# First 256 columns of x for the first 512 tokens: plain load and TensorE transposes in place of two crossbar pieces

## Chip, cores, metric

One core of one Trainium2 chip. The metric is the device time of one execution in microseconds (us), as the median of the executions. The profile counts from its own first instruction and ends a little earlier: its span is some 1.7 us below the device time of the same execution. In profile lines PE is TensorE (PEld its weight loads), DVE is VectorE, ACT is ScalarE, POOL is GpSimd, and SPq and ACTq are the queues from which the sync and scalar engines issue transfers. PSUM is the memory that TensorE's results land in.

## The reference, cut to what matters

```
x = A_x                                   # 2048 tokens x 1024, bf16
g = sigmoid((x * gate_w).sum(-1))
a = linear attention of x with A_wqkv (phi(t) = elu(t) + 1 + 1e-6), then @ A_wo
b = sliding-window attention of x (8 keys, every second token) with B_wqkv, then @ B_wo
return g * a + (1 - g) * b
```

All the work hangs on projections of x. The kernel feeds TensorE with x transposed (`xT`: features on partitions, tokens along the row). The very first projection is `k = x @ wk` of the linear attention; nothing useful can run on TensorE before the first piece of `xT` and of the weights `WkA` is there.

## The kernel before

All of x comes transposed through the DMA crossbar (`dma_start_transpose`). The first 512 tokens come in pieces of 256 columns, so that the projection can start on the first 256 columns:

```python
def load_xT(k, t0, t1):                      # crossbar: columns 256k..256k+255 of token tiles t0..t1-1
    nc.sync.dma_start_transpose(out=xT[:, 2 * k:2 * k + 2, t0 * P:t1 * P],
                                in_=rows(x, t0 * P, t1 * P)[:, 2 * k * P:(2 * k + 2) * P])

def load_wk(eng, k, h):                      # the weights for these columns, half h of the outputs
    eng.dma_start(out=WkA[h][:, 2 * k:2 * k + 2, :], in_=A_wqkv[2 * k * P:(2 * k + 2) * P, ...]...)

ones = nc.const_aps.tensor(1.0, [P, P], BF16)
load_wk(nc.scalar, 0, 0)
first_act = ...                              # a one-element activation
load_wk(nc.scalar, 0, 1)
load_xT(0, 0, 2)
load_xT(0, 2, 4)
for k in range(1, 4):
    load_wk(nc.sync, k, 0)
    load_xT(k, 0, 4)
    load_wk(nc.sync, k, 1)
...                                          # the other tiles of xT, then x as rows, other weights
mask = consts.tile([P, S // 2], BF16, name="mask")
nc.gpsimd.memset(mask[:], 1.0)
...  nc.gpsimd.affine_select(out=dst, in_=dst, ...)      # keeps or fills elements by position: the window's mask, needed much later
```

TensorE meanwhile multiplies ones by ones (warm-ups, to bring its clock up), then runs the projection in four groups `k` of 16 matmuls into 8 PSUM banks:

```python
warm_up(37)
first = [bank_k(i) for i in range(8)]
for k in range(4):
    for half in range(2):
        for t in range(4):
            for kt in (2 * k, 2 * k + 1):
                project(first[4 * half + t], t, kt, half)     # 128x128 weights, 512 columns moving
            ...
```

The softmax here doesn't subtract the row's maximum and nothing guards it: scores larger than these inputs give would overflow.

## Time and profile before

| | before |
|---|---|
| device time, median of 4 runs | 472.21 us (472.08 to 472.3) |
| span of the profiled execution | 470.9 us |
| warm-ups on TensorE | 0.84 to 4.95 us |
| first useful matmul | 5.35 us |
| GpSimd's first affine-select | 9.45 us |

The lines behind this table stand in the prediction below. How to read it: TensorE (PE in the profile) is busy nearly everywhere, so the time is the moment of its first useful matmul plus a nearly constant rest.

### The profile page before, as it was taken

To read this page: it belongs to the slowest core of one execution; us is meant where nothing else is said; L and a number is where in the kernel's file an instruction comes from. 1 tells how busy PE (TensorE), PEld (TensorE's weight loads), DVE (VectorE), ACT (ScalarE), POOL (GpSimd) and SP (SyncE) were. 2 spreads that over 40 slices of the span, in tenths; PEclk is the share of its full clock that TensorE was granted. 3 is DMA by queue.
4 is the path that set the end of the run, shared out by engine and by line. 5 is a ranking of instruction groups with operands and counts; after the bars stand their busy time and mean duration, and the time that the engine had idled before them with its cause. 6 is when DMAs were issued, how large, how long until landed. Compare 5 with 4: busy or idle time off the path is not lost.

```text
span 470.9 us, 13162 instructions
## 1 busy us (share of the span) xinstructions
PE 465.3 (99%) x5735; PEld 269.8 (57%) x5765; DVE 275.3 (58%) x598; ACT 169.1 (36%) x276; POOL 15.3 (3%) x30
## 2 busy tenths in 40 slices
PE   8999999999999999999999999999999999999997
PEld 5444444445444444444888888888874444444444
DVE  0596689990219999999666676767660049800000
ACT  1343321102433333334555555555553134221121
POOL 3300000500000000000000000000000000000000
PEclk9999999999999999999999999999999999999999
DMA  8999970000644233627325523442463923211001
GB/s 202 226 243 375 348 237 0 0 1 0 204 136 134 81 141 123 155 97 251 105 55 108 108 59 82 101 92 59 88 167 74 213 78 79 71 53 45 34 33 46
DMA packets 98732, 55.40 MB, mean 118 GB/s; under 512 B 70130, under 2 KB 90610, under 8 KB 98674
## 3 DMA queue, kind: packets, MB, share of 16 engines
q1 hardware_dynamic: 93378, 49.87, 39.9%
q10 hardware_dynamic: 5296, 4.69, 2.9%
q8 instruction: 45, 0.74, 0.6%
q14 instruction: 13, 0.11, 0.1%
HBM read 26.10 MB, written 15.86 MB: 89 GB/s over the span
## 4 chain that ended last, share of the span: by engine, by line
PE 86%; SPq 10%; DMA 2%; issue 1%; DVE 0%; DVEq 0%
PE q_ps L390 26%; PE d_ps L596 12%; PE p_ps L294 12%; PE e_ps L596 11%; PE g_ps L233 11%; PE p_ps L330 9%; SPq L115 4%; SPq L81 3%; DMA WvB<-in_B_wqkv_dram 2%; PE po L470 2%; PE s2b L448 2%; SPq L94 1%; SPq L98 1%; SPq L89 1%; SPq L119 1%
## 5 line engine op out<-in xcount | busy, mean ns | idle before, releaser
L390 PE MATMUL q_ps<-xT,WqB 64*64 64x512 bf16 x1024 | 70.3, 377 | 0.0
L390 PE MATMUL q_ps<-xT,WkB 64*64 64x512 bf16 x1024 | 69.8, 376 | 0.0
L156 DVE TENSOR_SCALAR e<-e 128x512 f32<-128x512 f32 x64 | 27.0, 423 | 68.3 <-ACT e L155 68.3
L294 PE MATMUL p_ps<-WvB,xT 128*128 128x512 bf16 x250 | 56.9, 379 | 0.3
L182 PE MATMUL pk_ps<-WkA,xT 128*128 128x512 bf16 x251 | 55.6, 381 | 0.7 <-DMA xT<-in_A_x_dram 0.4
L233 PE MATMUL g_ps<-pk,xrow 128*128 128x512 bf16 x251 | 55.2, 379 | 0.3
L453 ACT ACTIVATE PT<-s2b 128x928 bf16<-128x928 f32 (+4 forms) x40 | 34.2, 856 | 50.0 <-PE s2b L448 49.0
L455 DVE TENSOR_TENSOR PT<-PT,mask 128x928 bf16<-128x928 bf16 (+4 forms) x40 | 23.6, 590 | 36.3 <-ACT PT L453 36.3
L390 PEld LDWEIGHTS <-WkB 64*64 64x64 bf16 x1024 | 40.4, 107 | 6.9 <-DMA vd<-tmp 0.2
L330 PE MATMUL p_ps<-WqA,xT 128*128 128x512 bf16 x188 | 43.2, 379 | 0.3
L596 PEld LDWEIGHTS <-pqT 128*128 128x128 bf16 x272 | 26.0, 98 | 29.6 <-issue 0.2
L596 PEld LDWEIGHTS <-OBT 128*128 128x128 bf16 x272 | 26.0, 98 | 29.4
L182 PEld LDWEIGHTS <-xT 128*128 128x128 bf16 x256 | 25.1, 98 | 31.0 <-DMA xT<-in_A_x_dram 0.7
L390 PEld LDWEIGHTS <-WqB 64*64 64x64 bf16 x1024 | 39.4, 107 | 5.6 <-DVE qz L430 0.2
L233 PEld LDWEIGHTS <-xrow 128*128 128x128 bf16 x256 | 25.0, 98 | 30.2
L294 PEld LDWEIGHTS <-xT 128*128 128x128 bf16 x256 | 24.9, 98 | 30.2 <-issue 0.5
L603 DVE TENSOR_SCALAR osb<-e_ps,omg 128x128 bf16<-128x128 f32 x1 | 0.4, 351 | 57.6 <-PE e_ps L596 57.6
L155 ACT ACTIVATE e<-pk_ps 128x512 f32<-128x512 f32 x32 | 18.9, 597 | 40.6 <-PE pk_ps L182 36.4
L470 PEld LDWEIGHTS <-PT 64*56 64x56 bf16 (+2 forms) x1152 | 29.9, 104 | 4.5
L299 ACT CAST tmp<-p_ps 128x512 bf16<-128x512 f32 x32 | 18.7, 589 | 37.0 <-PE p_ps L294 26.6
L330 PEld LDWEIGHTS <-xT 128*128 128x128 bf16 x192 | 18.8, 98 | 22.6
L596 PE MATMUL d_ps<-WoA,pqT 128*128 128x512 bf16 (+1 forms) x133 | 30.7, 369 | 0.2
(63 smaller groups left out, 540.8 us busy)
## 6 DMA issues: line engine op xcount, KB each, us to landing
vd<-tmp SPq DMA_DIRECT2D x16, 264.0 KB
xrow<-in_A_x_dram SPq DMA_DIRECT2D x4, 1024.0 KB
out_dram<-osb ACTq DMA_DIRECT2D x31, 128.0 KB
pqd<-tmp SPq DMA_DIRECT2D x12, 256.0 KB
WvA<-in_A_wqkv_dram SPq DMA_DIRECT2D x2, 1024.0 KB
WoA<-in_A_wo_dram SPq DMA_DIRECT2D x2, 1024.0 KB
WvB<-in_B_wqkv_dram SPq DMA_DIRECT2D x2, 1024.0 KB
WqA<-in_A_wqkv_dram SPq DMA_DIRECT2D x2, 1024.0 KB
```

Source lines behind the costliest of these rows:

```text
L115: nc.sync.dma_start_transpose(out=xT[:, :, t * P:(t + 1) * P], in_=rows(x, t * P, (t + 1) * P))
L155: nc.scalar.activation(out=e[:], in_=pj[:], func=ACT.Exp)
L156: nc.vector.tensor_scalar(out=e[:], in0=e[:], scalar1=1.0, scalar2=1e-6, op0=ALU.min, op1=ALU.add)
L182: nc.tensor.matmul(pj[:], lhsT=xT[:, kt, t * P:(t + 1) * P], rhs=WkA[half][:, kt, :], start=(kt == 0), stop=(kt == KT - 1))
L233: nc.tensor.matmul(pj[:], lhsT=xrow[:, t, kt * P:(kt + 1) * P], rhs=pk[:, t, half * 512:(half + 1) * 512], start=(t == 0), stop=(t == NB - 1))
L294: nc.tensor.matmul(st["pj"][:], lhsT=xT[:, kt, t * P:(t + 1) * P], rhs=WvB[half][:, kt, :], start=(kt == 0), stop=(kt == KT - 1))
L330: nc.tensor.matmul(st["pj"][:], lhsT=xT[:, kt, t * P:(t + 1) * P], rhs=WqA[half][:, kt, :], start=(kt == 0), stop=(kt == KT - 1))
L390: nc.tensor.matmul(banks[o][64 * j:64 * j + 64, :], lhsT=lhsT(r, kt, j), rhs=rhs(r, kt), start=first and kt == 0, stop=kt == KT - 1, skip_ ...
L453: nc.scalar.activation(out=pt[:, :, 0:W_], in_=s2b[:].rearrange("p a b s -> p (a b) s")[:, :, 0:W_], func=ACT.Exp, scale=SCALE)
L455: nc.vector.tensor_tensor(out=pt[:, :, 0:W_], in0=pt[:, :, 0:W_], in1=mask[:, None, base:base + W_].broadcast_to([P, 4, W_]), op=ALU.mult)
L470: nc.tensor.matmul(o2[64 * h:64 * h + w, par, s_, i, :], lhsT=pt[r, i, o:o + w], rhs=V[r, m, 4 * c + i, :], start=True, stop=True)
L596: nc.tensor.matmul(st["ps"][:, 0:n], lhsT=lhsT, rhs=W[c0 // 512][:, c, c0 % 512:c0 % 512 + n], start=(side == 0 and c == 0), stop=(side == ...
```

## The change

Intent: get the first piece of `xT` without the crossbar. The first 256 columns of the first 512 tokens are loaded as plain rows; TensorE transposes them in eight 128x128 blocks against an identity matrix; DVE and ACT copy the blocks from PSUM into `xT`. The next crossbar piece goes ahead of the weights in the sync queue. Some warm-ups are taken out to make room. The diff, cut to its core (left out: a `load_rows` that takes a column range, so that the later load of these rows brings only the other 768 columns; one late weight load in two pieces):

```diff
     ones = nc.const_aps.tensor(1.0, [P, P], BF16)
+    pk = big.tile([P, NB, D], BF16, name="pk", tag="pkO")
+    ident = pk[:, NB - 1, 0:P]
+    nc.gpsimd.affine_select(out=ident, in_=ones, compare_op=ALU.is_equal, fill=0.0, base=0, pattern=[[1, P]],
+                            channel_multiplier=-1)
         load_wk(nc.scalar, 0, 0)
-        first_act = consts.tile([P, 1], BF16, name="first_act")
-        nc.scalar.activation(out=first_act[:], in_=ones[:, 0:1], func=ACT.Exp)
-        load_wk(nc.scalar, 0, 1)
-        load_xT(0, 0, 2)
-        load_xT(0, 2, 4)
-        for k in range(1, 4):
+        load_rows(nc.sync, 0, 4, 0, 2 * P)
+        load_xT(1, 0, 4)
+        load_wk(nc.sync, 0, 1)
+        load_wk(nc.sync, 1, 0)
+        load_wk(nc.sync, 1, 1)
+        for k in range(2, 4):
+            load_xT(k, 0, 4)
             load_wk(nc.sync, k, 0)
-            load_xT(k, 0, 4)
             load_wk(nc.sync, k, 1)
...
-            warm_up(37)
+            warm_up(33)
+            for t in (0, 2):
+                for kt in range(2):
+                    xt = ps_1.tile([P, 2 * P], BF16, name="xt_ps", tag="p1")
+                    for i in range(2):
+                        nc.tensor.transpose(xt[:, i * P:(i + 1) * P], xrow[:, t + i, kt * P:(kt + 1) * P], ident)
+                    (nc.scalar.copy if kt else nc.vector.tensor_copy)(out=xT[:, kt, t * P:(t + 2) * P], in_=xt[:])
```

More of the change, by code (lines that the diff above doesn't have):

```diff
@@ L86, with load_rows @@
     xrow = big.tile([P, NB, D], BF16, name="xrow", tag="vV")
-    def load_rows(eng, t0, t1):
-        eng.dma_start(out=xrow[:, t0:t1, :], in_=rows(x, t0 * P, t1 * P).rearrange("(t p) d -> p t d", p=P))
+    def load_rows(eng, t0, t1, d0=0, d1=D):
+        eng.dma_start(out=xrow[:, t0:t1, d0:d1],
+                      in_=rows(x, t0 * P, t1 * P)[:, d0:d1].rearrange("(t p) d -> p t d", p=P))
     WkA = [wpool.tile([P, KT, 512], BF16, name=f"WkA{h}", tag="wa") for h in range(2)]
@@ L115 @@
             nc.sync.dma_start_transpose(out=xT[:, :, t * P:(t + 1) * P], in_=rows(x, t * P, (t + 1) * P))
-        for t in range(0, NB, 4):
+        load_rows(nc.sync, 0, 4, 2 * P, D)
+        for t in range(4, NB, 4):
             load_rows(nc.sync, t, t + 4)
@@ L179 @@
             s1.enter_context(tc.manual_schedule(engines={DVE}))
-            pk = big.tile([P, NB, D], BF16, name="pk", tag="pkO")
             def project(pj, t, kt, half):
@@ L543 @@
             load_wo(1, 0, 4)
-            nc.sync.dma_start(out=WoB[1][:, 4:KT, :],
-                              in_=B_wo[4 * P:, 512:1024].rearrange("(k p) n -> p k n", p=P))
+            for k in (4, 6):
+                nc.sync.dma_start(out=WoB[1][:, k:k + 2, :],
+                                  in_=B_wo[k * P:(k + 2) * P, 512:1024].rearrange("(k p) n -> p k n", p=P))
             raw = wpool.tile([P, 4, D], BF16, name="raw", tag="wc")
```

## The prediction

> **What bounds the kernel now.** I read the page first, then the first 30 us in order of time, then the waits, then the last pieces of the chain. The page of the kernel before:
>
> ```profile
> span 470.9 us, 13162 instructions
> PE 465.3 (99%) x5735; PEld 269.8 (57%) x5765; DVE 275.3 (58%) x598; ACT 169.1 (36%) x276; POOL 15.3 (3%) x30
> PE   8999999999999999999999999999999999999997
> ...
> PE 86%; SPq 10%; DMA 2%; issue 1%; DVE 0%; DVEq 0%
> ```
>
> TensorE (PE) is busy in every slice and only the first and last slices are not full. The sum of its work is the span, so the change can act in two ways only: change how much PE does, or change when its first useful matmul starts. The list of PE waits shows that only the start is open (first for all of the run, then in the timeline of the start):
>
> ```profile
> PE warm L188 <- PEq L645: 0.8, 1, 0.8
> PE pk_ps L182 <- DMA xT<-in_A_x_dram: 0.4, 1, 0.4
> ```
>
> ```profile
> 0.80 0.95 POOL L129 MEMSET mask<- 128x1024 bf16 x1 [0.29 <-POOLq L645]
> ...
> 0.84 4.11 PE L188 MATMUL warm<-const-bfloat16-1.0 128*128 128x128 bf16 x37 [0.84 <-PEq L645]
> 1.69 0.14 POOL L141 MEMSET qsel<- 128x1 f32 x2
> ...
> 5.34 0.13 PEld L182 LDWEIGHTS <-xT 128*128 128x128 bf16 x2 [0.67 <-DMA xT<-in_A_x_dram]
> 5.35 24.99 PE L182 MATMUL pk_ps<-WkA,xT 128*128 128x512 bf16 x111 [0.40 <-DMA xT<-in_A_x_dram]
> ...
> 5.75 0.15 PEld L182 LDWEIGHTS <-xT 128*128 128x128 bf16 x1 [0.28 <-issue]
> 6.18 23.88 PEld L182 LDWEIGHTS <-xT 128*128 128x128 bf16 x111 [0.28 <-issue]
> ...
> 9.45 6.42 POOL L135 TENSOR_SCALAR_AFFINE_SELECT mask<-mask 64x64 bf16<-64x64 bf16 x15 [7.63 <-issue]
> ```
>
> Columns are start, duration, engine, line, operation, tiles and count, with the idle time before it. The reader is to see three things. PE multiplies constants (37 warm-up matmuls that produce nothing) from 0.84 to 4.95 us, then waits 0.40 us for the first crossbar piece of x, and does its first useful matmul at 5.35. After 6.18 it never waits. And GpSimd (POOL), which today has nothing to do with the start, stands idle from 1.83 to 9.45 us before its first affine-select although its input is ready: 7.63 us with the remark "issue", that is, nothing that the profile shows. At the end the chain is PE, then one small DVE evacuation:
>
> ```profile
> 467.23 0.91 PE e_ps L596 x16
> 468.14 0.04 DVEq L603
> 468.17 0.05 issue
> 468.22 0.35 DVE osb L603
> ```
>
> So: time = start of the first useful matmul (5.35) + about 463 us of dense PE + a fixed tail. A shift of the start goes through to the end one to one; I find no later wait that could swallow it. The most that an earlier start can bring is about 0.84 + 4.51 less what the first data need to arrive, and a quarter of a per cent is already 1.2 us.
>
> **What the Trainium skill says.** (1) "GPSIMD Engine Reference", section 2.1 Instruction dispatch: the GpSimd cores load kernel code at run time, and the first call into a freshly loaded kernel pays a load of some 6 us that no profile instruction shows. The trace agrees in kind and is longer: the 7.63 us above, in front of the first affine-select. In the built program an instruction that reloads the library stands just there, and the changed program has it in front of its very first affine-select. (2) "TensorE: Matmul & The Clock Gate", Part 1 (the HAM clock gate): PE runs at half clock until a free-running activity window of about 3.4 us has been busy, and falls back after an idle one. The trace agrees: 37 matmuls of 128 columns in 4.11 us are 111 ns each, while 111 of 512 columns in 24.99 us are 225 ns each, 56 ns per 128 columns; and the first useful loads start at 5.34, 5.75 and 6.18, so the first two useful matmuls still ran at the slow pace (about 0.41 us instead of 0.22, together 0.4 us lost). (3) The same page, Part 4 (PE-mode transpose): transposes do not count as busy for that gate. No row of the kernel before shows it, as it has none on PE. (4) "DMA: Bandwidth & Descriptors", Specifications: 512 B is the least run for full line rate. The plain load of 256 bf16 columns has runs of exactly 512 B, so it should not be penalised; no row of before has this size.
>
> **The change part by part.**
> Removed: two crossbar transposes of x (their issue held the sync queue from 0.81 to 3.42 us), a one-element activation, 4 of 37 warm-ups.
> Added: one plain load of 256 KB at 0.8 us; an identity made by an affine-select on POOL; 8 PE transposes; 4 copies of 128x256 out of PSUM, half on DVE, half on ACT.
> Moved: the next crossbar piece and the weights earlier in the sync queue by about 2 us. The second weight half goes from the ACT to the sync queue. Late weight halves in two pieces: 350 us later and with no wait there today, worth 0.
>
> Plain load: at 0.8 us with latency of issue about 2 us (the DMA slices of before are empty until about 2 us) and 512 KB of load and first weights at the 240 to 305 GB/s which the first slices reach, 1.7 to 2.2 us: x and the weights are there at about 4 us, 1.3 us earlier than today. If that were all: warm-ups end at 0.84 + 33 x 0.111 = 4.5; 8 transposes x 0.111 = 0.9 to 5.4; the first copies lie beside the later transposes; the first useful matmul at about 5.4, a draw with 5.35, later weights and pieces all in time.
>
> But in the program's order the first transpose waits for the identity. In the changed order POOL's first own act, at 0.80, is that library reload. Then the affine-select: 0.80 + 7.63 = 8.43. Its length from the POOL rows of 64 and 448 columns (234 and 611 ns, so 0.98 ns per column): 128 columns are 0.30 us. Identity at 8.73. The first two transposes and their result: 0.05 + 0.11 + 0.31 (a warm-up's own length) = 9.20. A DVE copy of 128x256 out of PSUM took 425 ns in before (float source): 9.63. The eight transposes, 8 x 0.111 from 8.78, end at 9.67 beside it. First useful matmul at about 9.65 instead of 5.35: **+4.3 us**, all on the path.
>
> The clock: warm-ups end at 4.5 to 4.7, PE is idle for about 4.1 us, longer than a window, so I expect PE cold again at 9.65. A full busy window from there ends 3.4 to 6.8 us later, on average 5.1; half of that is lost: 1.7 to 3.4, less the 0.4 us that before loses too: about +2.1. With 1 chance in 4 that no window was wholly idle and the clock stays up: -0.4. Weighted: **+1.5 us**.
>
> The library load may be as short as the skill's 6 us when it starts before the DMA traffic: then 1.6 us less. I take -0.4 for that on average. Sum: 4.3 + 1.5 - 0.4 = +5.4, that is 472.2 + 5.4 = 477.6. I put **477.5 us** on record, +1.1%.
>
> **The rivals.**
> Identity in time (1 in 8): the load of GpSimd's code may be a matter of where it stood, or already done before the start. For it: the author took just 4 warm-ups away, as if transposes would follow at once. Against it: 7.63 us of idle POOL with a finished input. It would make 471.6 to 472.6: +0.05 to +0.1 for the start, less up to 0.4 if the clock rises sooner.
> A wait late but clock warm: 475 to 476.5, if the gate sees the warm-up and forgets slowly.
> A late identity and a very cold clock, with transposes and waits for copies not counted as busy and the gate opening only at 16 us: 479 to 480.5.
> Queue order: weights behind the crossbar piece could be late for the second half of the first group, which comes 8 matmuls after the start. The issue of that load moves from 1.34 to about 2.6 us and it needs to land by 9.65 + 1.7 at the latest, or 7.1 in the early case; hidden anyway.
> PE work itself: 8 transposes for 4 warm-ups are +0.4 us only where identity is early; in the late case they are inside the sum above.
>
> **Range and chances.** Late identity with load of 6 to 7.6 us gives +2.7 to +4.3; the clock adds -0.4 to +3.0; so +2.3 to +7.3, 474.5 to 479.5. I widen a little above: 474.3 to 480.0 holds it 8 times in 10. The rest is mostly the early identity at 472. The 2% line is at 481.7 above and 462.8 below. The first would need a second long wait, the second cannot be, as at most 4.5 us lie before the first useful matmul. Faster 0.01, within 2% 0.95, slower 0.04.
>
> **What would show it.** In the profile after: POOL's affine-select to the identity starting at 7 to 8.5 us with an idle of 6 to 7.6 us; the transposes after 7.5 and named as waiting for POOL; PE nearly empty from 4.7 us on, a digit of 6 or less in the first slice; first useful matmul at 8 to 9.7; useful 512-column matmuls at 0.43 us each for several us; a PE sum and tail otherwise as now; all landings earlier than their use. I am wrong if the identity is there by 4.5 us, if the transposes start right behind the warm-ups, or if the shift at the start does not come back whole at the end.

## The result, and the profile after

The changed kernel takes 479.1 us (median of 4 runs, 478.9 to 479.33) against 472.21: 1.46% longer. Ratios here and below are taken over the runs of the same rounds; they go by means, so they are not quite the ratios of the medians. This one is 1.0146 (95% interval 1.0129 to 1.0164). Clear of noise it is slower by 6.9 us.

The page of the changed kernel:

```profile
span 477.6 us, 13206 instructions
...
PE   5999999999999999999999999999999999999997
...
PEclk8899999999999999999999999999999999999999
...
PE 97%; issue 2%; DVE 0%; POOL 0%; POOLq 0%; DVEq 0%
```

The loss is in the first slices: PE's first digit falls from 8 to 5, the granted clock (PEclk) now shows 8 in two slices where before it is 9 in all, and the rest is as full as before. (The clock's records begin with its first rise; the slow pace before that does not show in PEclk.) The chain of waits, which before went along the queue of DMA issues, now starts on GpSimd (start, duration, what):

```profile
0.91 0.01 POOLq L106
0.92 8.33 issue
9.26 0.29 POOL pk L106
9.55 0.04 issue
9.59 1.01 PE xt_ps L201 x8
```

Line 106 is the identity. For 8.33 us GpSimd waits for nothing that the profile shows, then makes the identity in 0.29 us, and PE's transposes follow at once. What stands ahead of the gap can be asked for by line; here the changed kernel's identity, then the affine-selects of the kernel before:

```profile
L106 POOLq MODIFY_POOL_CONFIG  x2: 11/11/11, 0.9 to 0.9; - x2
...
L135 POOLq MODIFY_POOL_CONFIG  x2: 12/12/12, 1.8 to 1.9; - x2
```

In every run this pair of instructions stands directly ahead of the first affine-select, and the memsets that go before it in the kernel before do not need it. That the gap behind it is a load of code is the prediction's reading; the profile shows the pair and the gap.

The timeline of the start:

```profile
0.84 3.65 PE L193 MATMUL warm<-const-bfloat16-1.0 128*128 128x128 bf16 x33 [0.84 <-PEq L657]
...
4.88 0.10 PEld L201 LDWEIGHTS <-xrow 128*128 128x128 bf16 x1 [0.63 <-DMA xrow<-in_A_x_dram]
...
9.26 0.28 POOL L106 TENSOR_SCALAR_AFFINE_SELECT pk<-const-bfloat16-1.0 128x128 bf16<-128x128 bf16 x1 [8.75 <-issue]
...
9.59 1.01 PE L201 MATMUL xt_ps<-pk,xrow 128*128 128x128 bf16 x8 [5.10 <-POOL pk L106]
...
10.40 9.78 PE L187 MATMUL pk_ps<-WkA,xT 128*128 128x512 bf16 x35
```

The rows of x are there at 4.88 (their first weight load into PE ends its wait for the DMA), but PE then stands for 5.10 us until the identity comes. The first useful matmul is at 10.40 instead of 5.35.

The second part of the loss is the clock. The windows of the changed kernel (stretch, its length, then busy time and count by engine, granted clock, DMA share, GB/s):

```profile
4.49:9.59 5.10, 0.00 (x0) 0.10 (x1) 0.00 (x0) 0.00 (x0) 0.34 (x2) 0.82 1.15 308
9.59:10.40 0.81, 0.81 (x9) 0.80 (x8) 0.29 (x1) 0.19 (x1) 0.81 (x2) 0.50 1.14 308
10.40:14.62 4.22, 4.22 (x13) 1.47 (x11) 0.29 (x1) 0.55 (x2) 4.09 (x13) 0.51 1.17 301
14.62:33.00 18.38, 18.38 (x87) 8.33 (x86) 8.63 (x17) 6.01 (x11) 2.87 (x11) 1.00 1.04 203
```

PE runs at half clock from the transposes until 14.6 us. By the starts of the matmuls in the trace, ten useful ones lie in 10.40 to 14.62, 0.42 us each, where ten at the full pace of 0.216 us take 2.16. In the records of the clock, it rose at 4.33 us, when the warm-ups were nearly over, fell at 7.74 in the middle of the wait, and rose again at 14.57.

The account, from the two profiled executions: the first useful matmul is 10.40 - 5.35 = 5.05 us later; the slow matmuls lose 4.22 - 2.16 = 2.06 us, of which the kernel before also loses 0.44 (its first three starts, 5.35 to 6.43, are 1.09 us where 0.65 would do). 5.05 + 2.06 - 0.44 = 6.67 us, and the spans differ by 477.6 - 470.9 = 6.7. Nothing later takes any of it back or adds to it: the next stage's first matmul (`g_ps`) starts at 61.04 us before and at 67.72 after, 6.68 later.

### The profile page after: what moved, and what is told of

Same layout as the page of the kernel before. It is cut to its first block, busy times and chain, and to the rows that moved or that the text cites. A ratio compares the mean times of both kernels' runs of the same rounds, so it can differ in the third digit from the quotient of the medians.

```text
span 477.6 us, 13206 instructions
## 1 busy us (share of the span) xinstructions
PE 468.9 (98%) x5769; PEld 270.3 (57%) x5769; DVE 275.9 (58%) x600; ACT 169.7 (36%) x277; POOL 15.6 (3%) x31
## 4 chain that ended last, share of the span: by engine, by line
PE 97%; issue 2%; DVE 0%; POOL 0%; POOLq 0%; DVEq 0%
PE q_ps L401 26%; PE pk_ps L187 12%; PE d_ps L608 12%; PE p_ps L305 12%; PE g_ps L244 12%; PE e_ps L608 11%; PE p_ps L341 9%; PE po L481 2%; PE s2b L459 1%; PE kv_ps L264 0%; PE w_ps L171 0%; PE xt_ps L201 0%; DVE osb L615 0%; POOL pk L106 0%; DVEq L615 0%
## 5 line engine op out<-in xcount | busy, mean ns | idle before, releaser
L187 PE MATMUL pk_ps<-WkA,xT 128*128 128x512 bf16 x256 | 57.5, 389 | 0.0
```

What stands on the lines that cost most here:

```text
L187: nc.tensor.matmul(pj[:], lhsT=xT[:, kt, t * P:(t + 1) * P], rhs=WkA[half][:, kt, :], start=(kt == 0), stop=(kt == KT - 1))
```

## The experiments

All ten give the right result, and all timed runs are in the fast state; run 4 is one profiled execution, its state unknown. They ran on three chips (runs 1 to 4, 5 to 8, and 9 and 10), each time with the kernel before in the same rounds. But the kernel before shows two levels in the new rounds: some 472.2 to 473.0 us, and in 7 of 33 runs some 474.3 to 474.8. The ratios, which go by means, are moved by this more than the medians, so I compare the lower levels where it matters and say so.

**1. Queue order and the rest, without the transposes.** From the changed kernel:

```diff
-    nc.gpsimd.affine_select(out=ident, ...)
-        load_rows(nc.sync, 0, 4, 0, 2 * P)
+        load_xT(0, 0, 2)
+        load_xT(0, 2, 4)
         load_xT(1, 0, 4)
         load_wk(nc.sync, 0, 1)
-            warm_up(33)  ... transposes and copies
+            warm_up(37)
```

> The changed kernel's queue order, its late weight halves and its missing one-element activation, but the first 256 columns of x come by the two crossbar pieces as before, 37 warm-ups, no identity and no transposes. Theory (late identity plus cold clock is all): 472.2 us, within 0.6 of the kernel before; first useful matmul at 5.2 to 5.6 us. Rival (the order of the queue brings weights or pieces late and costs part of the 6.9 us): 474 us or more, with PE waits for WkA or xT.

Measured: 474.03 us (lower level 473.9 to 474.2, one run at 475.9) against 472.53 (lower level 472.2 to 472.7); ratio 1.0022 (0.9997 to 1.0046). Against my expectation; about 1.6 us are lost between the lower levels, though the first useful matmul comes at 4.82 us, earlier than I expected. The timeline of this run shows where:

```profile
0.80 3.96 SPq L95 DMA_TRANSPOSE xT<-in_A_x_dram  x3
...
4.81 1.60 SPq L99 DMA_DIRECT2D WkA<-in_A_wqkv_dram  x3
...
8.82 0.81 PE L185 MATMUL pk_ps<-WkA,xT 128*128 128x512 bf16 x3 [2.10 <-DMA WkA<-in_A_wqkv_dram]
```

Three crossbar issues hold the sync queue (SPq) for 3.96 us, the second weight half is issued only at 4.81, and PE waits 2.10 us for it at the ninth matmul. So the rival is real for this program. It is not for the changed kernel, which has one crossbar issue ahead of that weight half (it is issued at 2.70 us) and no such wait in its profile. My experiment was badly cut: it put together two things that no kernel has together. Run 7 asks the question properly.

**2. The wait stays, the clock is kept up.**

```diff
-            warm_up(33)
+            warm_up(110)
```

> The changed kernel with 110 warm-ups in place of 33, so that PE is busy until about 8.7 to 10.3 us, when the identity comes. The wait for the identity stays, the cold clock after it goes. Theory (wait and clock are separate terms): identity still at about 9.5 us, useful matmuls at 216 ns each from the first on, the 10 slow matmuls and 8 slow transposes give back 2.1 + 0.4 us: 476.4 us (475.8 to 477.4, as the warm-ups may run past the identity). Rival (the clock is no term of its own; what matters is the wait alone): 479.1 us.

Measured: 477.31 us (476.77 to 477.6), ratio to before 1.0082 (1.0057 to 1.0107). In its timeline the warm-ups end at 8.72, and:

```profile
9.74 0.28 POOL L106 TENSOR_SCALAR_AFFINE_SELECT pk<-const-bfloat16-1.0 128x128 bf16<-128x128 bf16 x1 [9.24 <-issue]
...
10.07 0.61 PE L201 MATMUL xt_ps<-pk,xrow 128*128 128x128 bf16 x8 [1.35 <-POOL pk L106]
...
10.73 3.63 PE L187 MATMUL pk_ps<-WkA,xT 128*128 128x512 bf16 x16
```

The eight transposes take 0.61 us instead of 1.01 and 16 useful matmuls fit in 3.63 us. The identity happened to be later still (10.02), the first useful matmul at 10.73 is 5.38 us behind that of before, and there is no slow matmul: 5.38 - 0.44 = 4.94, and the span is 475.9 - 470.9 = 5.0 us longer. Against the changed kernel (479.1 and 479.2) some 1.8 us come back, of the 2.5 that I expected; the identity, 0.48 us later here, takes most of the rest. The clock is a term of its own. (This run's records of the clock are empty; the pace is what shows it.)

**3. The identity made on DVE.** A running sum gives the column number, a 32x32 transpose of it the row number within a block of 32, and four compares the identity. All of it lies in the part of `pk` that is not yet in use:

```diff
-    nc.gpsimd.affine_select(out=ident, in_=ones, ...)
+    nc.vector.tensor_tensor_scan(out=cnt, data0=ones, data1=ones, initial=0.0, op0=ALU.mult, op1=ALU.add)
+    nc.vector.transpose(out=pidx, in_=cnt[:, 0:32])
+    for b in range(4):
+        q = slice(32 * b, 32 * b + 32)
+        nc.vector.tensor_scalar(out=ident[q, :], in0=cnt[q, :], scalar1=pidx[q, 0:1], scalar2=32.0 * b,
+                                op0=ALU.subtract, op1=ALU.is_equal)
```

> The changed kernel with the identity made on DVE (a running sum, one 32x32 transpose, four compares, about 1.3 us from 0.8 us) in place of the affine-select on POOL; the result stays right. Theory: the identity is there at about 2.3 us, the transposes start when x lands, at 4.9 us, first useful matmul at about 5.7 us, 472.5 us (471.9 to 473.3). Rival (transposes and copies on PE, DVE and ACT, not the identity, cost the time): first useful matmul only at 7 us or later, 474 us or more.

Measured: 472.68 us, four runs at 472.61 to 472.72 and two at 474.72 and 474.87; ratio 1.0001 (0.9974 to 1.0028). The whole loss is gone, with transposes, copies and queue order untouched. So the identity's lateness was the cause. The profiled run is one of the two at the upper level. Its timeline:

```profile
1.54 1.23 DVE L112 TENSOR_SCALAR pk<-pk 32x128 bf16<-32x128 f32 x4
...
5.72 1.03 PE L207 MATMUL xt_ps<-pk,xrow 128*128 128x128 bf16 x8 [1.20 <-DMA xrow<-in_A_x_dram]
...
6.54 3.65 PE L193 MATMUL pk_ps<-WkA,xT 128*128 128x512 bf16 x10
```

The identity is done at 2.77 us and PE waits for the rows of x, not for it. x landed at 5.7 us here. In this run the clock rose only at 9.22 us, and the first six useful matmuls are slow.

**4. The load of GpSimd's code without DMA beside it.**

```diff
     nc.gpsimd.affine_select(out=ident, ...)
+    nc.gpsimd.memset(WkA[0][:, 0:1, 0:1], 0.0)      # the first load of the ACT queue must wait for this
+    nc.gpsimd.memset(xrow[:, 0:1, 0:1], 0.0)        # and that of the sync queue for this
```

> The changed kernel in which the first DMA of both queues waits until POOL has made the identity (POOL writes one element of their targets after it), so that the code load runs with no DMA of the kernel beside it. Not meant to be fast: about 483 us. If DMA traffic stretches the load, the time from the start of POOL's own work to the affine-select falls from 8.4 us to 7 us or less; if the load has a fixed length, it stays at 7.6 to 8.5 us.

Measured: 482.38 us, one run. The identity's line in the timeline:

```profile
8.51 0.28 POOL L106 TENSOR_SCALAR_AFFINE_SELECT pk<-const-bfloat16-1.0 128x128 bf16<-128x128 bf16 x1 [8.00 <-issue]
```

From 0.80, where GpSimd is free, to 8.51 are 7.71 us with no transfer of the kernel under way; the trace has no DMA packet at all in this stretch. So the load isn't long because of this kernel's DMA. The same stretch was 8.46 us in the changed kernel, 8.94 in run 2, 7.98 in run 5 and 7.87 in run 6: with transfers beside it, all four are longer, so DMA may still add to it; one execution doesn't tell. With transfers it varies by more than a microsecond between executions of equal start, and what sets it stays open. (In this run the wait of PE is put down to a mask instruction on GpSimd; PE's first transposes at 13.12 really follow the landing of x, issued at 8.91.)

**5. The wait alone, in the kernel before.** Crossbar pieces and order stay; the identity is made first on GpSimd and the last warm-up reads it:

```diff
+    nc.gpsimd.affine_select(out=ident, in_=ones, compare_op=ALU.is_equal, ...)
...
-                    nc.tensor.matmul(warm[:], lhsT=ones, rhs=ones, start=True, stop=True)
+                    nc.tensor.matmul(warm[:], lhsT=ones, rhs=ident if i == n - 1 else ones, start=True, stop=True)
```

> The kernel before with one part of the change alone: POOL makes the identity first, and the last of the 37 warm-ups reads it, so that PE waits for it. Crossbar pieces, queue order, no transposes, as before. Theory (the wait for the identity and the cold clock after it are the whole loss): identity at 8.6 to 9.7 us, first useful matmul some 0.1 us later, 8 to 12 useful matmuls at 427 ns: 477.5 to 479.5 us, as slow as the changed kernel less its 0.8 us of transposes and copies. Rival (transposes, copies or queue order carry a good part): 475.5 us or less.

Measured: 477.8 us (477.45 to 478.23) against 472.53, ratio 1.0106 (1.009 to 1.0122). Its timeline:

```profile
9.12 0.27 PE L191 MATMUL warm<-pk,const-bfloat16-1.0 128*128 128x128 bf16 x1 [4.28 <-POOL pk L105]
...
9.17 4.13 PE L185 MATMUL pk_ps<-WkA,xT 128*128 128x512 bf16 x10
```

One matmul that needs the identity and yields nothing costs 5.3 us (of the medians). First useful matmul at 9.17, 3.82 us late; nine slow starts up to 12.93 lose 3.76 - 9 x 0.216 = 1.82, less 0.44: 5.2 us in all, and the span is 476.1, 5.2 longer. Here the clock didn't fall during the wait: its first rise on record is at 12.82, and the first 36 warm-ups ran at the slow pace to their end (about 107 ns apart). So the slow matmuls after the wait don't depend on the clock having been up before it.

**6. The changed kernel again, on the chip of run 5.** No edit.

> The changed kernel once more, on the same chip as the run before this one and those after it: 478.9 to 479.4 us as on record, unless the code load is shorter or longer here; identity between 8.6 and 9.7 us.

Measured: 479.21 us (479.05 to 479.53), ratio 1.0137 (1.0116 to 1.0157), as expected. The difference to run 5 is 1.4 us. The identity ends at 8.95 here (9.06 in run 5), and from there to the first useful matmul are 0.86 us (0.11 in run 5): transposes and copies cost 0.75 us. The clock rose at 14.86 instead of 12.82, and twelve slow starts, 9.81 to 14.90, lose 5.09 - 12 x 0.216 = 2.50 us where run 5 lost 1.82: 0.68 more. -0.11 + 0.75 + 0.68 = 1.32, and `g_ps` starts at 67.56 against 66.23, 1.33 later. The spans differ by 477.6 - 476.1 = 1.5; the rest arises later, within the `q_ps` matmuls (222 to 363 us), and is not explained.

**7. The identity on DVE, with the queue order of before.**

```diff
         load_wk(nc.scalar, 0, 0)
+        load_wk(nc.scalar, 0, 1)
         load_rows(nc.sync, 0, 4, 0, 2 * P)
-        load_xT(1, 0, 4)
-        load_wk(nc.sync, 0, 1)
-        load_wk(nc.sync, 1, 0)
-        load_wk(nc.sync, 1, 1)
-        for k in range(2, 4):
-            load_xT(k, 0, 4)
+        for k in range(1, 4):
             load_wk(nc.sync, k, 0)
+            load_xT(k, 0, 4)
             load_wk(nc.sync, k, 1)
```

> As the run with the identity on DVE, but the weights and the crossbar pieces in the order of the kernel before, the second weight half on the ACT queue. Theory (the order is of no weight once the identity is in time): within 0.4 us of the run with the identity on DVE, about 472.6 us in its lower level. Rival (x's next piece ahead of the weights is what lets the plain load keep up): a PE wait for xT at the second group, 473.5 us or more.

Measured: 472.57 us (472.44 to 472.85), ratio 0.9996 (0.9982 to 1.0011); run 3's lower level was 472.6 to 472.7. The order moves the lower level by no more than 0.1 us. (Run 3 had two of six runs on the upper level and this one none; that is too few to tell whether the order matters for that.) This is a run of the lower level:

```profile
5.09 0.62 PE L204 MATMUL xt_ps<-pk,xrow 128*128 128x128 bf16 x8 [0.57 <-DMA xrow<-in_A_x_dram]
5.76 4.49 PE L190 MATMUL pk_ps<-WkA,xT 128*128 128x512 bf16 x20
```

x at 5.09, transposes at full clock (it rose at 4.70 us), first useful matmul at 5.76. Even with the identity in time the plain load and the transposes are no earlier than the crossbar's 5.35; what evens it out is that no useful matmul is slow.

**8. x and the first weights in two loads each, transposes in two parts.** On top of run 3, with 34 warm-ups in place of 33:

```diff
-        load_wk(nc.scalar, 0, 0)
-        load_rows(nc.sync, 0, 4, 0, 2 * P)
+        for kt in range(2):
+            nc.scalar.dma_start(out=WkA[0][:, kt, :], in_=A_wqkv[kt * P:(kt + 1) * P, D:D + 512])
+        load_rows(nc.sync, 0, 2, 0, 2 * P)
+        load_rows(nc.sync, 2, 4, 0, 2 * P)
...
+            for t in (0, 2):    # 4 transposes and their copies, then the 4 matmuls of tiles t and t+1, half 0
```

> The identity on DVE, the first x rows in two loads of two token tiles, the first weights in two loads, and the transposes of tiles 2 and 3 behind the first four useful matmuls. Theory (the landing of x and the eight transposes ahead of the first matmul are what is left): first useful matmul at 4.9 to 5.4 us instead of 5.7 to 6.5, 472.0 us (471.6 to 472.5), at best 0.1% below the kernel before. Rival (the plain load lands no earlier when split, as the queues share the same engines): 472.6 us or more.

Measured: 473.15 us (472.98 to 473.35), ratio 1.0008 (0.9994 to 1.0022): a miss in the time, by about 0.6 us against run 7.

```profile
4.42 0.63 PE L215 MATMUL xt_ps<-pk,xrow 128*128 128x128 bf16 x4
...
5.22 1.46 PE L195 MATMUL pk_ps<-WkA,xT 128*128 128x512 bf16 x4 [0.17 <-DVE xT L216]
...
6.52 0.39 PE L215 MATMUL xt_ps<-pk,xrow 128*128 128x128 bf16 x4
...
7.18 6.00 PE L195 MATMUL pk_ps<-WkA,xT 128*128 128x512 bf16 x27 [0.28 <-DVE xT L216]
```

The half load lands earlier (transposes at 4.42) and the first useful matmul is at 5.22, as I expected. But the fifth useful matmul is at 7.18, where run 7 has it at 6.64. Two things take the gain away. The second part has its copy delay in the open: PE goes from 6.52 to 7.18, 0.66 us, with four transposes and a wait for DVE; with all eight transposes ahead, later ones cover the first copies. And in this profile the first three useful matmuls ran at the slow pace: the first four took 1.30 us (5.22 to 6.52) where 0.86 would do, 0.44 lost, while run 7's clock was up at 4.70. Against run 7: -0.54 + 0.66 + 0.44 = 0.56 us, of the 0.6 measured. So the splitting alone is not shown to cost 0.6 us.

**9. and 10. More warm-ups.** In the kernel before, `warm_up(37)` becomes `warm_up(41)`; in run 7's kernel, `warm_up(33)` becomes `warm_up(39)`.

> The kernel before with 41 warm-ups in place of 37, so that PE has no 0.4 us gap before the first useful matmul (end of the issue at 5.2 us). Theory (the second level of the times, some 474.7 us, is the clock rising one window of 3.4 us later because the gap spoils a window): no run near 474.7, all at 472.1 to 472.8. Rival (the second level has nothing to do with the warm-up): runs near 474.7 in about one of four, as in the kernel before on the first of the two chips.

> The identity on DVE with the old queue order, and 39 warm-ups in place of 33, so that PE is busy until x lands at about 5 us. Theory (the same as for the 41 warm-ups): no run near 474.7, and 472.1 to 472.6, at best 0.1% under the kernel before. Rival: as the run with 33 warm-ups, 472.4 to 472.9, or slower where x lands before the 39 warm-ups end.

Measured: the kernel before with 41 warm-ups 472.43 us (472.34 to 472.55) against 472.58, ratio 0.999 (0.9973 to 1.0007); run 7's with 39, 472.87 us (472.39 to 473.89), ratio 1.0002 (0.9984 to 1.0019). None of the six runs with 41 is on the upper level, where before has 2 of 11 in the same rounds; at 7 of 33 in all rounds, six clean runs come by luck once in four times, so this fits the explanation and doesn't show it. The profiles speak against its simple form. If the clock changes at the ends of windows of 3.41 us (in the changed kernel it fell 7.74 - 4.33 = 3.41 us after it rose, and rose again 6.83, twice that, later), the window that ended with the rise at 6.25 in the kernel before began at 2.84 and held the whole gap of 0.40 us, and the clock rose all the same. In run 3, a run of the upper level, the window that ended at 9.22 - 3.41 = 5.81 held 1.20 us of idleness (x landed late), and the clock didn't rise at its end. So a longer gap, from a later landing of x, may be what makes the upper level; no profile of the kernel before is on that level, and it stays open. The 39 of the DVE kernel gave a spread and no gain: the expectation of 472.1 to 472.6 was missed. In its profile PE was busy without a gap from 0.84, and the clock was up only at 6.36, so that transposes and the first useful matmul were slow. No version beats the kernel before by more than the noise; the best, with 41 warm-ups, is 0.1% below it with an interval across 1.

## Why the prediction was right

The measured 479.1 us lies in the range, 1.6 us above the 477.5. By its steps:

- **PE's start sets the time, and a shift goes through whole.** Right: 5.05 + 1.62 us at the start are 6.7 us at the end. The paces it read from the lines are a little too slow (111 and 225 ns; by the starts of neighbouring matmuls they are 107 and 216), as the sums hold the last one's tail and some records of matmuls are missing. Nothing rests on the difference.
- **The identity is late because GpSimd first reloads its library.** That the late identity is the cause is right, and shown from both sides: the wait alone in the kernel before costs 5.3 us (run 5), and the identity made elsewhere brings the changed kernel back to 472.7 (run 3). That the delay is a reload fits the pair of MODIFY_POOL_CONFIG ahead of it; no run takes the pair away, so this part is argued.
- **Its size.** Sized too small. The predicted stretch was 7.63 us, less 0.4 for a load without DMA traffic beside it; measured were 8.46 us. The credit was not earned: even with quiet queues the stretch was 7.71 (run 4). This term is 1.2 of the 1.6 us by which the prediction fell short. The affine-select itself (0.30 predicted, 0.28 measured) and the way from the identity to the first useful matmul (0.92 predicted, 0.86 measured) were right. Two of the signs named in advance lay outside their ranges for this reason: the affine-select started at 9.26, not at 7 to 8.5, and the first useful matmul at 10.40, not at 8 to 9.7.
- **The clock.** The mechanism is right: PE is cold again after the wait, and run 2 gives this term back alone. That 1.62 measured is so near to +1.5 is luck: +1.5 was a mean over two branches, and the one that came true had been put at +2.1, half a microsecond too much. Without the weights and the credit, the prediction's own steps give 4.3 + 2.1 = 6.4, nearer to the 6.9 measured than the 5.4.
- **Plain load early, at about 4 us.** Too early for PE's wait, which ends at 4.88 us in the changed kernel and at 5.1 to 5.7 in the others with one load whose wait shows. The data themselves were nearly in time: in the packed traces the last 512-byte packet of x ends at 4.24 us in the changed kernel, 4.25 in run 3 and 4.45 in run 7, and PE's wait ends 0.64, 1.47 and 0.64 us after it. That last stretch was not in the sum, and what sets it stays open. Hidden in the changed kernel. It is the reason why run 3 has nothing to win: I put 5.4 us for the first useful matmul with the identity in time, and saw 5.76 and 6.54.
- **Queue order hidden anyway.** Right for the changed kernel (no PE wait for weights), and run 7 shows it neutral; run 1, with two crossbar issues in place of the plain load ahead of the weights, has a PE wait of 2.10 us and loses 1.6.
- **The rivals.** Identity in time, the one-in-eight case, did not happen. A late identity with a warm clock is what run 2 made: predicted 475 to 476.5, measured 477.3, again by the longer load. The measured 479.1 lies in the range of the rival "very cold clock" (479 to 480.5), but not for its reason: that rival had the clock up only at 16 us, and it was up at 14.57.

## What to carry to other kernels

Before putting an operation of an idle engine on the critical path, look at what stands before its first use in the trace: 7.6 us of unexplained idleness in front of GpSimd's first affine-select cost nothing before, and a gap of the same kind 6.7 us after, with the half clock that followed the wait. Where an operand is needed in the first microseconds, make it with instructions that the trace shows running at once (here six small DVE instructions, done at 2.77 us), and count the wait's second price, the matmuls that run at half clock after it. And when several steps each have a latency, keep work behind them: splitting the transposes brought the first useful matmul forward by 0.54 us and left a copy delay in the open.

## What the Trainium skill lacked or had wrong

- "GPSIMD Engine Reference", section 2.1 Instruction dispatch, gives some 6 us (5.95 measured there) for the load before the first call into freshly loaded code. Here the stretch from the moment GpSimd is free to its first affine-select was 7.7 us without the kernel's DMA, 7.9 to 8.9 us at the head of the program with it, and 7.3 to 8.4 us behind memsets in the kernel before and in runs 1, 3, 8 and 9; in the two DVE-identity runs with the old order it was 10.65 and 10.00 us. The page doesn't say which operations need it: memsets ran at 0.80 us before it, the affine-select did not.
- "TensorE: Matmul & The Clock Gate", Part 1, agrees: the clock rose at 4.33, fell 3.41 us later at 7.74 and rose at 14.57 us. The page says that the number of slow matmuls varies from run to run with the phase of the window; how much idleness a window may hold and still count as busy it does not say. Here 0.40 us of 3.41 did not keep the clock down (the kernel before), and 1.20 us did (run 3). Nor does it have the two levels of the times: run 3 took 474.72 us when the clock rose at 9.22 us, and run 7, the same but for the queue order, 472.68 when it rose at 4.70; but in run 3 x also landed 0.63 us later (5.72 against 5.09). That the phase of the window is the cause is argued from these two profiles, not shown.
- The same page, Part 4 (PE-mode transpose), gives some 275 to 390 ns for one transpose. Here one took 311 ns at half clock (the changed kernel) and 218 at full clock (run 2; ends are modelled). In a row of eight they came every 0.107 us at half clock, and every 0.056 once the clock was up (0.61 us together in run 2): they do run at the full clock. Whether they count as busy for the gate no run here separates.
- "DMA: Bandwidth & Descriptors", Specifications, has 512 B as the least run for full rate; no figure there covers what mattered, the time from issue to use of a 256 KB load in such runs beside 256 KB of weights and a crossbar piece: 4.08 us in the changed kernel (0.80 to 4.88, of which 0.64 after its last packet) and 4.2 us with nothing before it (8.91 to 13.12, run 4).
